# A written-out order searched anew: exponentials over four banks, block 0 normalised by VectorE, 20 leading products

## The chip, the cores and the metric

The kernel runs on one core of a Trainium2 chip. The metric is device time in microseconds of one execution. Every time before the change comes from three timed runs and from one profiled execution of the same program. In the profile PE is TensorE, PEld its weight loads, ACT ScalarE, DVE VectorE, POOL GpSimd and SP SyncE, which issues all the DMAs here.

## The reference

One transformer block on 2048 tokens of width 640, in bfloat16. Attention works in four segments of 512 tokens, with 32 heads of width 20; between the segments runs a compressive memory. Cut to what matters:

```python
h  = x + A(layernorm(x))
h2 = h + silu(layernorm(h) @ w1) @ w2          # w1: 640 x 1728, w2: 1728 x 640

# A: q, k, v = x @ wq, x @ wk, x @ wv, split in heads and in 4 segments of 512
for s in range(4):
    p     = softmax(q_s @ k_s.T / sqrt(20) + causal_mask)
    a_dot = p @ v_s
    a_mem = (phi(q_s) @ M) / (phi(q_s) @ z + 1e-6)   # phi(t) = t + 1 if t > 0 else exp(t)
    o_s   = sigmoid(beta) * a_mem + (1 - sigmoid(beta)) * a_dot
    M += phi(k_s).T @ v_s ;  z += phi(k_s).sum(0)
return concat(o_s) @ wo
```

## The kernel before

Tokens lie in 16 blocks of 128, four to a segment. Every piece of work is a named *task* with the engine instructions that it issues. The function `build` declares all the tasks; then `schedule` walks `ORDER`, a fixed list of 1462 entries, and appends each task to the instruction stream of its engine in the order of the list. Nothing is decided at run time: each engine runs its own stream in order, and a tracker sets the semaphore waits between engines wherever a task reads or overwrites what another one wrote. An entry reads `name/mark:slots`. The slots are the buffers that the task takes, in the order in which it declares them; the mark picks the engine or the form: A ScalarE, D VectorE, G GpSimd, S SyncE, and C the *column form* of a product. Without a mark the task goes to the first engine that it was declared for, which is ScalarE for evictions of PSUM.

A product in the column form (`mms`, line 549) is written as four products of 32 output columns each, side by side in the array; without the mark it is one product of 128 (line 548). The scores (line 946) use row tiles instead: heads are 20 wide, and four heads run in four row strips. The products of probabilities and values (line 994) and of the memory (line 1112) are always in column tiles.

PSUM has eight banks of 512 columns. The names of the tasks, with s the segment, b a block, c a chunk of five:

- `x0`, `x1`, `x2` load blocks 0, 1 and 2 to 3 (line 581); `w_q0` and the like load weights (584). All are in SP's queue, in the order of the list.
- `fill25` is 25 products on zeros that nothing reads (620), `fill5` five more.
- `n1_st`, `n1_rs`, `n1_ap` are the first layer norm of a block: two half-row sums and an aggregation on VectorE (753, 756; block 1's sums are made on ScalarE, 744 to 748), the reciprocal root on GpSimd (763, 765), and the normalising itself, on VectorE (781), for block 0 on ScalarE (777) with a product of mean and root from GpSimd (768) ahead of it. `n1_tp`, `n1_te` transpose blocks 0 to 3 on TensorE and evict them (791, 800); later blocks use a DMA transpose (`n1_tr`, 806).
- `re_q`, `re_k` rearrange the weights of queries and keys (711). `pr{s}{c}{w}` are the projections of queries (w 0) and keys (w 1), `qe` their evictions (876 on ScalarE, 877 on VectorE), `ex`, `pa`, `pb` the function phi (883, 890, 896). `v` and `ve` are the values and their eviction (842 on ScalarE, 843 on VectorE).
- Group g of segment s has the number k = 8s + g, with four heads. `qk{k}a0`, `qk{k}b0`, `qk{k}e0` are *score visits*: the scores of four heads into two pairs of banks. `e{k}a0` and `e{k}a2` are the exponentials of the first and the second pair, 1024 columns each (959), `mk` the causal mask on GpSimd (971), `av` the product with the values, `oe` its eviction (1008 on ScalarE, 1010 on VectorE), `tm`, `td`, `nm`, `ad` the memory part, the transposition, and the normalising (1044 to 1072).
- `kt`, `mz`, `ma`, `mb` update the memory; `vt` gathers the rows of groups 5 to 7.
- `ot`, `wo`, `rs`, `n2_*` are the output projection, the residual and the second layer norm; `h1_{s}_{f}_0.{z}`, `th`, `s` the first layer of the MLP with its activation (1211 on ScalarE, 1217 on VectorE); `h2`, `o`, `out` the second layer, the sum and the store.

The scores and their exponentials as they stand (lines 940 to 962):

```python
sca = [G.alloc("ps", 2) for _ in range(nr // 2)]      # two pairs of banks
...
for q0 in range(r0, r0 + nr, 2):
    scp = sca[(q0 - r0) // 2]
    def e_ex(eng, q0=q0, scp=scp):
        b0 = scp.slot
        T.add(AC, lambda e: e.activation(out=pt[:, pta.slot, q0:q0 + 2, 0:width],
                                         in_=sc3[:, b0:b0 + 2, 0:width], func=ACT.Exp, scale=SCALE), ...)
    G.task(f"e{name}{q0}", {AC: act_c(2 * width)}, e_ex, [(scp, [0])], [(pta, [q0])], ...)
```

## Time and profile before

| | |
|---|---|
| timed runs | 295.88, 297.27, 298.88 us; median 297.27 |
| profiled execution | span 293.9 us from the first to the last instruction; the page gives no time of its own beside the span |
| TensorE busy | 282.0 us, 96% of the span, 4365 products and as many weight loads |
| VectorE, ScalarE, GpSimd busy | 218.6 (74%), 216.5 (74%), 148.1 us (50%) |
| exponentials of the scores | 160, 154.1 us, 1.027 us each |
| granted TensorE clock | full in all 40 slices of the page |
| HBM | read 10.41 MB, written 2.62 MB |

How to read it: "busy" adds up the time in which an engine runs an instruction, over the whole span. A stage in which one engine is full sets its pace by that engine, whatever the mean is; so the stretches of 20 us are read beside the page. A group of instructions shows its line, engine, operation, output and inputs with their shapes, the count, the busy time in all and the mean of one in ns, then the idle time ahead of it and what ended that. "issue" is time in which an engine waited for nothing that the profile shows. Instructions of one engine that follow each other closely overlap a little, so a piece of several is shorter than its count times the mean.

### The profile page before, as it was taken

To read this page: it belongs to the slowest core of one execution; us is meant where nothing else is said; L and a number is where in the kernel's file an instruction comes from. 1 tells how busy PE (TensorE), PEld (TensorE's weight loads), DVE (VectorE), ACT (ScalarE), POOL (GpSimd) and SP (SyncE) were. 2 spreads that over 40 slices of the span, in tenths; PEclk is the share of its full clock that TensorE was granted. 3 is DMA by queue.
4 is the path that set the end of the run, shared out by engine and by line. 5 is a ranking of instruction groups with operands and counts; after the bars stand their busy time and mean duration, and the time that the engine had idled before them with its cause. 6 is when DMAs were issued, how large, how long until landed. Compare 5 with 4: busy or idle time off the path is not lost.

```text
span 293.9 us, 10138 instructions
## 1 busy us (share of the span) xinstructions
PE 282.0 (96%) x4365; PEld 159.8 (54%) x4365; DVE 218.6 (74%) x456; ACT 216.5 (74%) x281; POOL 148.1 (50%) x294
## 2 busy tenths in 40 slices
PE   6899889999999999999999899999999999999996
PEld 5454435445644445566654554656664657754574
DVE  3999888899997678798899835877746776635613
ACT  7699999999999899977789857979979640005400
POOL 6759675686947545746748432348638321300000
PEclk9999999999999999999999999999999999999999
DMA  7947869635464200453543402403320031450003
GB/s 212 342 120 186 113 176 186 167 69 108 87 80 113 73 2 3 53 99 70 91 122 92 93 2 21 81 2 57 73 25 2 2 70 22 91 156 0 3 0 112
DMA packets 48604, 24.83 MB, mean 84 GB/s; under 512 B 38896, under 2 KB 47472, under 8 KB 48560
## 3 DMA queue, kind: packets, MB, share of 16 engines
q1 hardware_dynamic: 48560, 24.19, 38.1%
q8 instruction: 34, 0.56, 0.8%
q14 instruction: 10, 0.08, 0.1%
HBM read 10.41 MB, written 2.62 MB: 44 GB/s over the span
## 4 chain that ended last, share of the span: by engine, by line
PE 83%; DVE 7%; ACT 6%; DMA 1%; issue 1%; POOL 0%; SPq 0%; ACTq 0%; DVEq 0%
PE ps_all L548 49%; PE ps_all L549 20%; PE ps_all L946 8%; ACT PT L959 5%; PE ps_all L994 5%; DMA x_tok<-in_A_x_dram 1%; PE ps_all L1198 1%; DVE xn_rot L781 1%; DVE oTs L1010 1%; DVE phiQ L890 1%; DVE stt L753 1%; PE ps_all L1112 1%; DVE Vx L843 1%; DVE otok L1046 1%; DVE QK L877 0%
## 5 line engine op out<-in xcount | busy, mean ns | idle before, releaser
L959 ACT ACTIVATE PT<-ps_all 128x1024 bf16<-128x1024 f32 x160 | 154.1, 1027 | 16.2 <-PE ps_all L946 15.1
L971 POOL TENSOR_SCALAR_AFFINE_SELECT PT<-PT 128x512 bf16<-128x512 bf16 x128 | 82.8, 651 | 63.9 <-ACT PT L959 60.5
L1211 ACT ACTIVATE th<-ps_all 128x512 f32<-128x512 f32 (+1 forms) x56 | 31.7, 589 | 38.1 <-PE ps_all L548 23.7
L1217 DVE SCALAR_TENSOR_TENSOR sT<-th,ps_all 128x512 bf16<-128x512 f32 (+1 forms) x56 | 36.0, 661 | 17.0 <-ACT th L1211 16.4
L548 PE MATMUL ps_all<-w_sb,sT 128*128 128x320 bf16 x324 | 46.3, 299 | 0.1
L548 PE MATMUL ps_all<-tT,w_sb 128*128 128x512 bf16 x178 | 41.4, 380 | 0.0
L548 PEld LDWEIGHTS ps_all<-w_sb,sT 128*128 128x128 bf16 x324 | 31.0, 98 | 13.2 <-issue 0.6
L753 DVE BATCH_NORM_STATS2 stt<-x_tok 128x6 f32<-128x320 bf16 x62 | 27.1, 478 | 3.8 <-DMA x_tok<-in_A_x_dram 3.6
L1072 POOL TENSOR_TENSOR otok<-on 128x320 bf16<-128x320 bf16 x24 | 19.7, 824 | 17.5 <-DVE on L1064 17.5
L1254 DVE SCALAR_TENSOR_TENSOR x_tok<-ps_all,x_tok 128x640 bf16<-128x640 f32 (+1 forms) x17 | 13.3, 784 | 17.9 <-PE ps_all L548 13.1
L548 PEld LDWEIGHTS ps_all<-tT,w_sb 128*128 128x128 bf16 x178 | 16.5, 98 | 18.7 <-issue 0.6
L877 DVE CAST QK<-ps_all 128x512 bf16<-128x512 f32 x25 | 17.1, 685 | 8.6 <-PE ps_all L548 4.7
L1010 DVE TENSOR_SCALAR oTs<-ps_all,lsc 128x512 bf16<-128x512 f32 x26 | 19.3, 741 | 2.6 <-PE ps_all L994 2.2
L549 PE MATMUL ps_all<-tT,w_sb 128*32 128x512 bf16 x328 | 20.5, 380 | 0.0
L1064 DVE TENSOR_TENSOR on<-ps_all,rd 128x640 bf16<-128x640 f32 x24 | 19.8, 824 | 0.8
L765 POOL TENSOR_TENSOR rst<-rst,eps_c 128x1 f32<-128x1 f32 x32 | 18.3, 573 | 2.5
L549 PE MATMUL ps_all<-w_sb,sT 128*32 128x320 bf16 x496 | 18.8, 300 | 0.0
L781 DVE TENSOR_SCALAR xn_rot<-x_tok,mvt,rst 128x640 bf16<-128x640 bf16 x31 | 16.1, 534 | 3.3 <-POOL rst L765 2.8
L548 PE MATMUL ps_all<-tT,wkr 128*128 128x512 bf16 (+1 forms) x77 | 18.4, 367 | 0.0
L548 PE MATMUL ps_all<-wv_sb,tT 128*128 128x320 bf16 x115 | 18.0, 300 | 0.5 <-ACT PT L959 0.3
L763 POOL TENSOR_TENSOR rst<-mvt,eps_c 128x1 f32<-128x1 f32 x32 | 6.7, 209 | 22.5 <-DVE mvt L756 21.8
L994 PE MATMUL ps_all<-PT,Vx 128*32 128x512 bf16 (+3 forms) x384 | 17.4, 301 | 0.0
(111 smaller groups left out, 403.1 us busy)
## 6 DMA issues: line engine op xcount, KB each, us to landing
out_dram<-x_tok SPq DMA_DIRECT2D x15, 160.0 KB, 1.9
w_sb<-in_B_w_dram SPq DMA_DIRECT2D x5, 432.0 KB, 4.1
x_tok<-in_A_x_dram SPq DMA_DIRECT2D x3, 640.0 KB, 4.4
w_sb<-in_B_w_dram SPq DMA_DIRECT2D x3, 480.0 KB, 4.0
QKV<-QK SPq DMA_DIRECT2D x12, 72.0 KB
wv_sb<-in_A_wv_dram SPq DMA_DIRECT2D x1, 800.0 KB, 8.2
wo_sb<-in_A_wo_dram SPq DMA_DIRECT2D x1, 800.0 KB, 5.3
w_sb<-in_B_w_dram SPq DMA_DIRECT2D x1, 640.0 KB, 6.0
```

The costliest lines, as they stand in the source:

```text
L548: return [lambda e: e.matmul(out, lhsT=lhsT, rhs=rhs, start=start, stop=stop)]
L549: return [lambda e, p=p: e.matmul(out[p:p + 32, :], lhsT=lhsT[:, p:p + 32], rhs=rhs, start=start, stop=stop, tile_position=(0, p)) for p i ...
L753: T.add(DV, lambda e, hh=hh: e.bn_stats(out=stt[:, s, 6 * hh:6 * hh + 6], in_=xb[:, 320 * hh:320 * hh + 320]), reads=R((xa, xsub)), writes ...
L946: fns.append(lambda e, j=j, o=o, r=r, q0=q0, q1=q1, qa=qa, ka=ka: e.matmul(ps_all[:, o:o + q1 - q0], lhsT=ka[32 * r:32 * r + DH, 128 * j:1 ...
L959: T.add(AC, lambda e: e.activation(out=pt[:, pta.slot, q0:q0 + 2, 0:width], in_=sc3[:, b0:b0 + 2, 0:width], func=ACT.Exp, scale=SCALE), re ...
L971: fns.append(lambda e, v=v: e.affine_select(out=v, in_=v, pattern=[[0, 4], [1, 128]], compare_op=ALU.is_ge, fill=0.0, base=0, channel_mult ...
L994: fns.append(lambda e, j=j, r=r, h=h, pa=pa, pt=pt, co=co, q0=q0, ji=ji: e.matmul(bank(po)[32 * r:32 * r + 32, q0:hi], lhsT=vtile(vx)[:, j ...
L1010: f = lambda e: e.tensor_scalar(out=o, in0=i_, scalar1=lsc[:, g:g + 1], scalar2=None, op0=ALU.mult)
L1064: T.add(DV, lambda e: e.tensor_tensor(out=on[:, ona.slot, :, :].rearrange("p b (x e) -> p b x e", e=DH), in0=v[:, :, :, 0:DH], in1=r2.unsq ...
L1072: T.add(PO, lambda e: e.tensor_tensor(out=o_dst, in0=on[:, ona.slot, 0, :].rearrange("p (i x) -> p i x", i=4), in1=on[:, ona.slot, 1, :].r ...
L1211: T.add(AC, lambda e: e.activation(out=th[:, tha.slot, lo:hi], in_=bank(ps)[:, lo:hi], func=ACT.Tanh, scale=0.5), reads=R((ps, [0])), writ ...
L1217: T.add(DV, lambda e: e.scalar_tensor_tensor(out=sT[:, f, lo:hi], in0=th[:, tha.slot, lo:hi], scalar=1.0, in1=bank(ps)[:, lo:hi], op0=ALU. ...
```

## The change

Four edits, none in the arithmetic of the result:

1. `ORDER` is another list of 1448 entries. The tasks are the same.
2. A new mark W. A score visit whose exponential has it runs one activation over its two pairs of banks, 2048 columns, through an address pattern with the distance of the pairs, and the entry of the other half goes. The pairs are taken in the order of their slots, by the scores too. 14 visits have it: e0b0, e7b2, e13a0, e13b2, e14a0, e14b0, e15a0, e16a0, e21a0, e23b0, e24b2, e24e2, e29a2, e29b0.
3. Block 0's normalising has only VectorE's form; ScalarE's, and GpSimd's product for it, are gone.
4. `fill20` stands in the place of `fill25`.

The diff, cut to its core; of the list the start, a part of segment 0, and a part of segment 1:

```diff
 class Graph:  # schedule
-            t.cols = eng == "C"
-            t.eng = {"A": AC, "D": DV, "G": PO, "S": SP, "C": PE}[eng] if eng else list(t.engs)[0]
+            t.cols, t.whole = eng == "C", eng == "W"
+            t.eng = {"A": AC, "D": DV, "G": PO, "S": SP, "C": PE, "W": AC}[eng] if eng else list(t.engs)[0]
             assert t.eng in t.engs and (t.alt or not t.cols)
-            for a in t.allocs:
+            both = [t]
+            if t.whole:
+                m = todo.pop(name[:-1] + ("2" if name[-1] == "0" else "0"))
+                assert not any(self.tasks[p].name in todo for p in m.preds), name
+                both.append(m)
+            for a in [a for q in both for a in q.allocs]:
...
 ORDER = """
-epsc:0 iota halfc zpad warm:0 x0:0 mt2 n1_st0:4 mt3 mt0 mt1 mta1 mtb1 vpad1 x1:1 n1_st1/A:1,2 x2:2,3 w_q0:0 w_q1 w_k0
-vpad0 fill25:0 n1_rs0 n1_ap0/A:1 sel n1_tp0:2 fill5:7 n1_te0/A:1 n1_st2/D:5,3 mta0 n1_rs1 n1_st3:0 n1_rs2 w_k1 w_wv:0
-n1_rs3 re_wk4/G:0 mtb0 mm4 n1_ap1 n1_tp1:0 n1_ap2 n1_tp2:4 n1_ap3:0 n1_tp3:2 re_wq0/D:0 n1_te1/A pr000x.0:6 re_wq0h/D
+zpad:0 warm:0 x2:11,10 halfc iota mt3 epsc mta3 x0:7 n1_st0:6 sel x1:8 n1_st1/A:5,3 n1_rs0 n1_rs1 n1_st2:2,0 n1_rs2
+fill20:1 n1_ap0:1 n1_tp0:3 fill5:7 n1_te0:0 n1_st3:1 n1_rs3 n1_ap1 n1_tp1:6 n1_te1 n1_ap2 n1_tp2:3 n1_te2 w_k0:0
+re_wk0/G:0 w_k1 n1_ap3:1 n1_tp3:0 n1_te3 w_q0 re_wq0:0 pr000x.0/C:5 w_q1 re_wq2/G mt0 mt2 mta0 re_wk3/G re_wq4/G
+re_wq1/A re_wk0h re_wq0h re_wk1 pr001x.0/C:7 pr001x.1/C pr000x.1/C re_wk2 pr001y.0/C:6 pr001y.1/C pr000y.0/C:1
+pr000y.1/C pr011.0/C:2 qe000x:0 qe001x/D qe001y pa001:1 re_wq3 qe000y qk0a0:3,6 pr011.1/C qe011/D:0 ex001:1 beta
+w_wv:0 lsc0 e0a0:4 zf0 zf1 pr010.0/C:0 pr010.1/C qe010/D e0a2 qk0b0:2,4 e0b0/W:0 pr021.0/C:1 pr021.1/C qe021:0
...
+n1_st6:5 ex021:1 ex011:0 vt06:0 kt00:4 vt00 w_w1_4 qk1a0:5,2 e1a0:2 pr041.0:7 pr041.1 qe041/D:0 e1a2 v02.0:4 v02.1
+ve02 qk1b0:1,6 e1b2:5 e1b0 pb011 n1_ap5:3 n1_tr5:1 pa021:0 pb021 n1_ap7:2 mm4 mk0b mk0a mzc4 n1_rs4 n1_ap4:0 vt09
...
+s0_2_0 pa141:2 pb141 qk13a0:0,2 e13a0/W:6 h1_0_4_0.0:5 pr231.0:7 h1_0_4_0.1 th0_4_0:0 s0_4_0 pb140 pr231.1 qe231/D:0
+qk13b0:2,0 e13b2/W:1 h1_0_3_0.0/C:4 h1_0_3_0.1/C th0_3_0:0 mk12a mk12b mk12e av12:5 oe12/D:0 w_w2_1 kt12:1 kt14:3
...
     def layer_norm(tag, b, xa, xsub, dstA, i, prio):
-            if first:
-                T.add(PO, lambda e: e.tensor_scalar(out=nmr[:, s, :], in0=mvt[:, s, 0:1], scalar1=rst[:, s, :], scalar2=-1.0,
-                                                    op0=ALU.mult, op1=ALU.mult),
-                      reads=R((st, ["mv", "r"])), writes=R((st, ["n"])))
...
-            if eng == AC:
-                T.add(AC, lambda e: e.activation(out=xn_rot[:, xn.slot, :], in_=x_tok[:, b % 12, :], func=ACT.Identity,
-                                                 scale=rst[:, s, :], bias=nmr[:, s, :]),
-                      reads=R((xa, xsub), (st, ["r", "n"])), writes=R((xn, [0])))
-                return
...
-        G.task(f"{tag}ap{b}", {DV: 0.46, AC: 0.70} if first else {DV: 0.46}, e_apply,
-               [(xa, xsub), (st, ["mv", "r", "n"] if first else ["mv", "r"])], [(xn, [0])], prio)
+        G.task(f"{tag}ap{b}", {DV: 0.46}, e_apply, [(xa, xsub), (st, ["mv", "r"])], [(xn, [0])], prio)
...
     def scores(name, pool, pt, blocks, pr, width=L, sub=WH):
+                ets = []
+
+                def rank(sca=sca, ets=ets):
+                    if any(t.whole for t in ets):
+                        return sorted(sca, key=lambda a: a.slot)
+                    return sca
...
-                    def e_ex(eng, q0=q0, scp=scp):
+                    def e_ex(eng, q0=q0, scp=scp, rank=rank, ets=ets):
+                        if any(t.whole for t in ets):
+                            a, b = rank()
+                            src = bass.AP(tensor=ps_all, offset=512 * a.slot,
+                                          ap=[[4096, 128], [512 * (b.slot - a.slot), 2], [512, 2], [1, width]])
+                            o = pt[:, pta.slot, 0:4, 0:width].rearrange("p (a b) x -> p a b x", a=2)
+                            T.add(AC, lambda e: e.activation(out=o, in_=src, func=ACT.Exp, scale=SCALE),
+                                  reads=[("ps", z.slot + q) for z in (a, b) for q in range(2)], writes=R((pta, [0, 2])))
+                            return
```

More of the change, by code (lines that the diff above doesn't have):

```diff
@@ L229 @@
     __slots__ = ("name", "engs", "emit", "reads", "writes", "prio", "mode", "allocs", "preds", "npred",
-                 "succ", "ready", "lat", "start", "end", "eng", "idx", "bw", "cols", "alt")
+                 "succ", "ready", "lat", "start", "end", "eng", "idx", "bw", "cols", "alt", "whole")
 class Graph:
@@ L253, in task @@
         t = Task()
-        t.cols, t.alt = False, alt
+        t.cols, t.alt, t.whole = False, alt, False
         t.name, t.emit, t.mode, t.lat, t.bw = name, emit, mode, lat, bw
@@ L318, in schedule @@
             assert not slots, name
-            for a in t.allocs:
-                a.users -= 1
+            for q in both:
+                for a in q.allocs:
+                    a.users -= 1
             order.append(t)
@@ L368 @@
-pr011.0:2 pr011.1 re_wk3/D qe001x/A re_wq4/G qk0a0:0,3 ex001:0 pa001:0 pb001 kt00:2 pr021.0:7 pr021.1 e0a2:4 qe011/D:0
-qe021/D:0 e0a0 pr010.0:6 vpad2 w_w1_0/S pa021:1 n1_st4:3 pr010.1 qe010/D pa011:2 n1_st5:0 ex011:1 pb011 kt01:3
-qk0b0:4,2 w_w1_2/S e0b2:5 e0b0 v00.0/C:0 pr020.0/C:7 pr020.1/C mk0a qe020/A v00.1/C n1_rs5 vt09:0 zf0 vt03 n1_st7:1
-n1_rs7 qk0e0:2,4 v01.0:6 v01.1 e0e2:2 v02.0:4 e0e0 ve01/D:0 zf1 v02.1 n1_ap5:0 n1_tr5:2 ve00/A vt00 qk1a0:6,1 ex021:1
-pr031.0:3 pr031.1 ve02/D n1_st6:7 lsc0 e1a0:1 n1_rs4 n1_ap4:1 e1a2 qe031/D:0 qk1b0:6,4 v03.0:0 lsc1 lsc2 lsc3
@@ new lines @@
+pr101.0/C:4 pr101.1/C e6b0 qk6e0:0,2 e6e2:1 e6e0 mm5 mk5a vpad1 mm7 mm0 mk5b av5:7 mm3 mzc7 mz01:5 n1_tr8 qe101/D mz04
+mz00 mz02 mz03 ma0:0 pr111.0/C:4 qk7a0:5,2 e7a0:3 e7a2 oe5/D:1 pr111.1 qe111/D pr130.0:0 pr130.1 qe130/D:0 qk7b0:4,6
+e7b2/W:0 ex100:1 v13.0/C:1 mk6a mzc0 n1_rs9 n1_ap9:0 mm1 mzc1 mk6e mzc5 mk6b n1_tr11 w_w2_0 w_w1_2 td5/C:3 nm5:3
+w_wo:0 n1_tr9 mk7a v13.1/C ve13/D av6:0 qk8a0:3,5 e8a0:4 e8a2 mk7b oe6/D:0 pa101:1 pr140.0:7 pr140.1 qe140/D:0 av7:4
+oe7/D:1 qk8b0:0,2 e8b0:2 e8b2 mk8b mm6 mb00:0 mk8a td6/C:6 nm6:2 pr131.0/C:7 td7/C:4 nm7:1 qk8e0:5,0 e8e0:6 pr131.1
@@ L509, in build @@
     rst = sb("rst", [128, pools["st"], 1], F32)
-    nmr = sb("nmr", [128, pools["st"], 1], F32)
     eps_c = sb("eps_c", [128, 2], F32)
@@ L733, in layer_norm @@
         xn = G.alloc("xn")
-        first = tag == "n1_" and b < 1
         if tag == "n1_":
```

197 lines of the change are left out of this document (96 added, 101 removed).

## The prediction

> **What bounds the kernel now.** I read the page's engine line first, then the stretches of 20 us. The columns of a stretch are its length, then the busy time of TensorE (PE), its weight loads, VectorE, ScalarE and GpSimd, the granted clock, and the DMA share.
>
> ```profile
> span 293.9 us, 10138 instructions
> PE 282.0 (96%) x4365; PEld 159.8 (54%) x4365; DVE 218.6 (74%) x456; ACT 216.5 (74%) x281; POOL 148.1 (50%) x294
> ...
> 0.00:20.00 20.00, 16.40 (x171) 10.13 (x172) 14.44 (x47) 15.34 (x24) 13.42 (x47) 1.00 0.77 241
> 20.00:40.00 20.00, 17.66 (x258) 8.93 (x256) 17.39 (x40) 19.44 (x25) 15.32 (x34) 1.00 0.69 123
> 40.00:60.00 20.00, 18.98 (x407) 9.16 (x399) 18.12 (x38) 19.33 (x23) 12.90 (x25) 1.00 0.85 188
> 60.00:80.00 20.00, 19.43 (x405) 11.06 (x398) 19.28 (x45) 19.10 (x24) 15.45 (x37) 1.00 0.49 91
> 80.00:100.00 20.00, 19.87 (x383) 9.87 (x385) 16.73 (x33) 18.56 (x25) 12.16 (x21) 1.00 0.50 103
> 100.00:120.00 20.00, 19.84 (x338) 9.40 (x330) 15.41 (x29) 19.25 (x26) 10.98 (x17) 1.00 0.01 3
> ...
> 160.00:180.00 20.00, 18.99 (x285) 10.37 (x278) 13.04 (x28) 14.64 (x21) 7.42 (x14) 1.00 0.23 47
> ...
> 280.00:294.00 14.00, 11.29 (x84) 7.90 (x81) 3.45 (x5) 0.00 (x0) 0.00 (x0) 1.00 0.17 59
> ```
>
> TensorE is busy for 96% of the span. By stretches it lacks 3.6 us of the first twenty, 2.3 of the second, 1.0 of the third, 0.6, 0.1 and 0.2 of the next three, 1.0 at 160 to 180, and 2.7 at the end, where the last output leaves. ScalarE is the engine that is full from 20 to 120 us: 19.4, 19.3, 19.1, 18.6 and 19.3 of 20. So up to some 60 us ScalarE sets the pace and TensorE waits for it; from 60 to 120 us both are full; behind that TensorE alone decides. A new order can win only what TensorE waits, at most 3.4 us between 20 and 60 us and about 2 behind, or less TensorE work.
>
> **TensorE's work.** The chain that ended last shows what a visit costs, and what a change of tiling costs (start, length, then the work).
>
> ```profile
> 42.76 1.19 PE ps_all L549 x20
> ...
> 62.40 1.19 PE ps_all L548 x5
> ...
> 100.17 1.08 PE ps_all L549 x20
> ...
> 104.63 2.27 PE ps_all L549 x40
> ...
> 154.75 2.26 PE ps_all L548 x10
> ```
>
> L548 are full products, L549 the same work in four column tiles (the mark C). Five full products of 512 columns behind other tiling take 1.19 us, ten take 2.26, so 1.07 for five and 0.12 for the change. Twenty column products take 1.19 behind scores and 1.08 behind the value visits, which are column products too; forty take 2.27. Both forms cost the same, and a change of tiling costs 0.11. Counted from the two lists, TensorE runs the same 508 visits beside the filler; 291 instead of 121 of them are in column form, and the changes of tiling fall from 173 to 167: six times 0.11 is 0.7 us less at most. I take 0.6.
>
> [...] The sum keeps equal cost.
>
> **ScalarE's work.** The groups by shape, then one piece of the chain.
>
> ```profile
> L959 ACT ACTIVATE PT<-ps_all 128x1024 bf16<-128x1024 f32 x160 | 154.1, 1027 | 16.2 <-PE ps_all L946 15.1
> ...
> L1211 ACT ACTIVATE th<-ps_all 128x512 f32<-128x512 f32 x52 | 30.3, 604 | 35.6 <-PE ps_all L548 23.7 <-DVE sT L1217 11.4 <-PE ps_all L549 0.4
> ...
> L883 ACT ACTIVATE ex<-QK 128x512 bf16<-128x512 bf16 x25 | 15.5, 630 | 1.2 <-DVE phiQ L896 1.2
> ```
>
> ```profile
> 37.24 3.79 ACT PT L959 x4
> ```
>
> An exponential over 1024 columns takes 1.027 us, one activation over 512 takes 0.604: 0.423 per 512 columns. Four in a row take 3.79, so 0.948 each: 0.08 overlap. Over 2048 columns I estimate 1.027 + 2 x 0.423 = 1.873, and 1.79 in a row, against 1.90 for two: 0.10 less each, 1.4 us for all 14. No row shows four banks in one instruction. At best it saves 0.10; if the address pattern over two pairs cost as much as a start, it saves nothing. I take 0.10. It frees the first pair of banks 0.85 us later; where the lists have such a visit, the next scores on those banks stand behind some 2 us of other products, which cover that. Two of the 14 (e0b0, e7b2) lie before 60 us, where ScalarE decides: 0.2 us. The other twelve lie where TensorE is full; they win between 0 and 1.2, and I take 0.2.
>
> **The start.** The order in time of the first 14 us.
>
> ```profile
> 0.80 1.35 SPq L581 DMA_DIRECT2D x_tok<-in_A_x_dram  x3
> ...
> 1.12 4.32 PE L620 MATMUL ps_all<-zpad 128*128 128x256 bf16 x25 [1.12 <-DVE zpad L599]
> ...
> 3.10 0.89 DVE L753 BATCH_NORM_STATS2 stt<-x_tok 128x6 f32<-128x320 bf16 x2 [2.03 <-DMA x_tok<-in_A_x_dram]
> ...
> 3.59 0.74 ACT L744 ACTIVATE xn_rot<-x_tok 128x640 bf16<-128x640 bf16 x1 [0.23 <-DMA x_tok<-in_A_x_dram]
> ...
> 4.02 0.21 DVE L756 BATCH_NORM_AGGREGATE mvt<-stt 128x2 f32<-128x12 f32 x1
> 4.15 0.17 DVE L642 TENSOR_SCALAR ident<-iot 128x128 bf16<-128x128 int32 x1
> ...
> 5.61 0.92 ACT L777 ACTIVATE xn_rot<-x_tok,nmr,rst 128x640 bf16<-128x640 bf16 x1
> ...
> 5.88 0.88 DVE L753 BATCH_NORM_STATS2 stt<-x_tok 128x6 f32<-128x320 bf16 x2 [1.56 <-DMA x_tok<-in_A_x_dram]
> ...
> 6.58 0.45 PE L791 MATMUL ps_all<-ident,xn_rot 128*128 128x128 bf16 x5 [1.14 <-ACT xn_rot L777]
> ...
> 7.08 0.19 POOL L763 TENSOR_TENSOR rst<-mvt,eps_c 128x1 f32<-128x1 f32 x1 [0.56 <-DVE mvt L756]
> 7.35 0.55 POOL L765 TENSOR_TENSOR rst<-rst,eps_c 128x1 f32<-128x1 f32 x1
> ...
> 9.22 0.45 DVE L781 TENSOR_SCALAR xn_rot<-x_tok,mvt,rst 128x640 bf16<-128x640 bf16 x1 [0.51 <-POOL rst L765]
> ...
> 10.08 0.71 PE L548 MATMUL ps_all<-tT,wqr 128*128 128x256 bf16 x5
> ...
> 13.47 0.39 PE L946 MATMUL ps_all<-w_sb 20*128 20x512 bf16 x4
> ...
> 13.92 1.94 ACT L959 ACTIVATE PT<-ps_all 128x1024 bf16<-128x1024 f32 x2 [0.26 <-PE ps_all L946]
> ```
>
> Now block 0 is in at 3.1 us, block 1 at 3.6, blocks 2 and 3 at 5.9. After the change the double load goes first and block 0 is the third block of four in the same queue: in between 3.6 and 5.9, and I take 4.7; block 1 then ends at 5.9. VectorE's list begins with the sums of block 0 and cannot pass them: 0.89 + 0.21 from 4.7 to 5.8, the identity (0.17) to 6.0, block 2's sums to 7.1. Only then comes the normalising of block 0, now on VectorE (0.45), to 7.5. ScalarE's 0.92 at 5.61 and GpSimd's product ahead of it go. Block 3's sums end at 8.6. Block 1's, on ScalarE, took 3.59 to 5.61 and now run from 5.9 to 7.9; its reciprocal root ends at 8.7, and those of blocks 2 and 3 stand behind it on GpSimd at 0.19 + 0.55 each, to 9.4 and 10.2. So block 3 is normalised at 10.6 instead of 9.67, 0.9 later, and the first projection starts near 11.0 instead of 10.08. The weights aren't late: the key weights take the place of the query weights, and the value weights move behind. The first scores need all four evictions of projection 0; ScalarE has the last transposes and a rearranging (re_wq1, 640 columns, so about the 0.92 of the row at 5.61) ahead of two of them. I walk that to 14.2 for the scores (13.47 now) and 14.7 for the first exponential (13.92): **0.8 us late**. Bounds: 0.3, if block 0 is in at 4.2, and 1.4, if at 5.3.
>
> Then one gap on ScalarE. In the new list the eviction ve02 stands between the second and third exponential of group 1, and its products stand behind the scores qk1a0, pr041 and v02.
>
> ```profile
> 19.34 2.82 PE ps_all L548 x20
> ```
>
> ```profile
> 22.32 0.24 ACT L646 ACTIVATE bsel<-beta_bc 128x32 f32<-128x32 bf16 x1
> ...
> 22.54 3.77 ACT L959 ACTIVATE PT<-ps_all 128x1024 bf16<-128x1024 f32 x4
> ```
>
> Twenty value products take 2.82, so 0.70 a half; five projections 1.08; v02 ends 1.1 + 1.4 = 2.5 us behind qk1a0. ScalarE's two exponentials fill 1.9 (now four run on for 3.77). It idles some 0.6 us, and the two exponentials behind it wait. It can't be below nothing; at most it is 0.9. Up to the ninth group of scores (some 58 us) ScalarE also gets one eviction of 512 columns more (qe021, 0.5) and loses lsc0 (0.2) and one exponential of L883's kind (ex101, 0.5 in a row); with the two joined visits, 0.4 less. So the ninth group is +0.8 + 0.6 - 0.4 = **1.0 us late**. From there TensorE has the same work in both lists, and the delay stays.
>
> The rest I cost at nothing. VectorE and GpSimd swap rearrangings and evictions; VectorE has 17.4 and 18.1 of 20 us between 20 and 60, and its list to that point differs by under 1 us by my count, so if it became the bound it would be late, or early, by as much. SP issues x4, w1_3 and x8 ahead of the first transposed keys, which nothing reads before the memory products behind the sixth group of scores (mz01). Removing five leading products costs TensorE nothing while it waits for block 0; what it costs if that cover is gone is the third rival.
>
> **Instructions.** The column form has four products and four loads where the full form has one.
>
> ```profile
> q8 instruction: 34, 0.56, 0.8%
> ```
>
> ```profile
> 167.53 0.11 PEld L946 LDWEIGHTS ps_all<-QKV 20*128 20x128 bf16 x5 [0.21 <-issue]
> ...
> 168.79 0.10 PEld L946 LDWEIGHTS ps_all<-QKV 20*128 20x128 bf16 x3 [1.15 <-issue]
> ```
>
> The first row is from the page's queues: 34 packets, 0.56 MB, 16 KB each. The program's 4365 products and as many loads come to 8730 instructions; 34 packets are one for each 257. The other two rows are a pause of 0.9 us inside one score visit, with no engine to wait for ("issue", longer than the load's own 0.1): I read it as a late refill. After the change there are 6592 products by my count of the lists, 51 packets, one each 5.5 us instead of 8.3. I take one more pause, 0.9 us; between none and five (4.5).
>
> **Sum.** Start and gap +1.0, tilings -0.6, late joined visits -0.2, refills +0.9, other waits behind 60 us as now: +1.1 us. The profiled execution's span is 293.9, so 295.0 after; the median of the three runs, 297.27, stands 3.3 above the span, and I carry the difference over: 298.4 us.
>
> **Rivals.** (1) **The waits go**: the new list feeds TensorE through its waits. For it: 2.3 and 1.0 us of idle between 20 and 60 us, 1.0 at 160 to 180, and less ScalarE work in that part. Against it: ScalarE is full there, and the late start moves it as a whole. If block 0 is in at 4.2, the gap closes and 3.4 us of waits go: +0.3 - 0.4 - 0.8 - 3.4 = -4.3, 293.0. [...] Five pauses more instead of one: +4.7, 302.0. (3) **The clock falls** between the leading products and the first transposes. The first products ran slower (25 of 256 columns take 4.32 us, 0.17 each; 512 columns take 0.214 later, so 256 take 0.107); the granted clock is 1.00 in every stretch. Twenty end near 4.7, the first transposes come at 7.5: 2.8 us without a product, against 1.1 now. If the clock halves, the projections ahead of the first scores (10.08 to 13.47) take up to 3.4 us longer: +4.5, 301.8. [...] (4) **Joined visits cost as much as two**: +0.4, 298.8, inside the forecast.
>
> [...]
>
> **How the numbers follow.** Forecast 0.57 (with rival 4), waits go 0.16, refills 0.17, clock 0.10. The forecast's own range is 296.0 to 300.5, from its bounds; the whole range reaches to 293.9 and 302.0. One per cent is 3.0 us, about what a measurement can tell from no change: faster is under 294.3, slower over 300.2. Of the forecast 0.03 is over that, so slower is 0.30; of the first rival 0.13 is under it; the rest, 0.57, is within.
>
> **What would show it.** The start: block 0's sums begin at 4.2 to 5.3, first scores near 14.2, first exponential near 14.7. The joined visits: 14 rows of 2048 columns near 1.87 us. ScalarE idles before ve02. TensorE's busy time stays near 282, with 51 instruction packets; pauses marked "issue" inside visits show refills. A clock under full in the first 20 us shows rival 3. I am wrong if TensorE's idle between 20 and 60 us falls under 2 us, or if idle behind 60 us doubles.

## The result, and the profile after

The changed kernel takes 308.11 us in the median (307.73 to 308.59), against 298.07 us (295.88 to 299.03) for the kernel before on the same chip: a ratio of 1.0366, 95% interval 1.0309 to 1.0424. It is 10 to 11 us slower, where I had said 298.4 and no measurable change. The profiled execution spans 306.9 us, 13.0 more than the one before.

From the page of the kernel after: the engine line, the granted clock in 40 slices, and the queue of the instructions.

```profile
span 306.9 us, 14572 instructions
...
PE 285.4 (93%) x6582; PEld 169.4 (55%) x6592; DVE 219.1 (71%) x451; ACT 217.4 (71%) x270; POOL 147.8 (48%) x295
...
PEclk9799986999999999999999999999999999999999
...
q8 instruction: 52, 0.85, 1.2%
```

VectorE, ScalarE and GpSimd are busy within 1 us of before, TensorE for 285.4 us instead of 282.0, with products at half clock among them. What grew most is the time in which TensorE waits, and the clock is no longer full: it is at 7 tenths in the second slice and at 8 and 6 in the sixth and seventh. The stretches of 20 us (length, then the busy time of TensorE, its loads, VectorE, ScalarE and GpSimd, the clock, the DMA share, GB/s):

```profile
0.00:20.00 20.00, 15.48 (x217) 9.50 (x217) 12.35 (x39) 13.67 (x23) 10.62 (x39) 0.91 0.75 245
20.00:40.00 20.00, 17.89 (x267) 9.26 (x264) 18.03 (x44) 18.78 (x24) 14.80 (x34) 1.00 0.54 87
40.00:60.00 20.00, 17.35 (x373) 8.07 (x364) 13.68 (x28) 16.19 (x18) 12.85 (x30) 0.83 0.58 102
60.00:80.00 20.00, 17.18 (x318) 8.93 (x321) 16.32 (x35) 17.34 (x20) 11.76 (x27) 1.00 0.72 152
80.00:100.00 20.00, 17.38 (x415) 10.22 (x405) 17.72 (x36) 17.82 (x25) 13.38 (x27) 1.00 0.59 102
100.00:120.00 20.00, 19.36 (x464) 9.26 (x466) 15.45 (x28) 17.37 (x18) 9.97 (x15) 1.00 0.27 61
```

From 40 to 100 us TensorE lacks 2.7, 2.8 and 2.6 us, where it lacked 1.0, 0.6 and 0.1. ScalarE, full there before, now has 2 to 4 us idle in each. So the two engines no longer hold each other up at full pace: something else ends their waits. The list of what TensorE waited for (us in total, times, longest), six of its rows:

```profile
PE ps_all L786 <- DVE xn_rot L777: 3.3, 3, 1.7
PE ps_all L556 <- issue: 2.1, 3, 1.4
PE ps_all L948 <- DMA QKV<-w_sb: 1.9, 1, 1.9
...
PE ps_all L948 <- DVE Vx L838: 1.1, 1, 1.1
...
PE ps_all L556 <- DMA sT<-otok: 1.0, 1, 1.0
PE ps_all L948 <- issue: 0.7, 2, 0.6
```

and the one row of before that answers to "issue":

```profile
PE ps_all L946 <- issue: 0.9, 1, 0.9
```

Three places carry much of what was lost, and each has its own cause.

**The start.** The order in time of the first 16 us:

```profile
4.34 0.89 DVE L759 BATCH_NORM_STATS2 stt<-x_tok 128x6 f32<-128x320 bf16 x2 [3.27 <-DMA x_tok<-in_A_x_dram]
...
6.97 0.45 PE L786 MATMUL ps_all<-ident,xn_rot 128*128 128x128 bf16 x5 [1.40 <-DVE xn_rot L777]
...
9.67 1.38 PE L786 MATMUL ps_all<-ident,xn_rot 128*128 128x128 bf16 x10 [1.71 <-DVE xn_rot L777]
...
10.78 0.45 DVE L777 TENSOR_SCALAR xn_rot<-x_tok,mvt,rst 128x640 bf16<-128x640 bf16 x1 [0.50 <-POOL rst L771]
...
12.06 0.83 PE L556 MATMUL ps_all<-tT,wqr 128*32 128x256 bf16 x12
...
15.50 0.40 PE L948 MATMUL ps_all<-w_sb 20*128 20x512 bf16 x4
...
15.94 1.02 ACT L969 ACTIVATE PT<-ps_all 128x1024 bf16<-128x1024 f32 x1
```

The first projection starts 2.0 us later than before (10.08), the first exponential too (13.92). Part of it is the clock, which comes next.

**The clock.** The trace tells when the granted clock changes: in the profile after at 9.70, 13.11, 43.83 and 50.66 us, each a whole number of times 3.41 us from the others. Busy time and clock of TensorE (second number, and the clock ahead of the last two) in single periods of 3.41 us between such times:

```profile
6.29:9.70 3.41, 1.03 (x11) 0.72 (x12) 2.04 (x7) 2.35 (x6) 1.44 (x5) 1.00 1.04 365
9.70:13.11 3.41, 3.11 (x38) 2.23 (x41) 2.77 (x10) 2.44 (x5) 3.33 (x11) 0.50 0.78 253
40.42:43.83 3.41, 1.86 (x45) 0.83 (x36) 2.66 (x6) 2.90 (x4) 2.80 (x7) 1.00 0.23 42
43.83:47.24 3.41, 2.49 (x22) 1.06 (x27) 1.44 (x4) 1.94 (x2) 1.56 (x3) 0.50 0.78 184
47.24:50.65 3.41, 3.41 (x31) 0.96 (x31) 2.19 (x6) 2.49 (x3) 2.96 (x9) 0.50 1.12 223
```

A period with TensorE busy for 1.03 of 3.41 us is followed by one at half clock, a period with 1.86 by two. The mean clock of all four timed executions was 0.982 or 0.983, so each had three such periods. In the second case a wait of 1.9 us stands behind it. SyncE's queue and the scores that wait:

```profile
23.91 0.51 SPq L591 DMA_DIRECT2D w_sb<-in_B_w_dram  x1
26.88 1.22 SPq L801 DMA_TRANSPOSE tT<-xn_rot  x1
...
34.30 4.17 SPq L903 DMA_DIRECT2D QKV<-w_sb  x6
38.52 1.20 SPq L801 DMA_TRANSPOSE tT<-xn_rot  x1
39.76 1.36 SPq L903 DMA_DIRECT2D QKV<-w_sb  x2
41.16 2.44 SPq L1111 DMA_TRANSPOSE phiKt<-phiK  x1
...
44.41 0.40 PE L948 MATMUL ps_all<-w_sb 20*128 20x256 bf16 x4 [1.89 <-DMA QKV<-w_sb]
```

Twelve gathers `vt` (L903) must land before `qk4e0` and the groups behind it can run. SyncE issues without a break from 26.88 to 49.3 us, at 0.7 us for a gather and 1.2 for a transpose, and the last gather leaves at 41.1. Ahead of that it stood still from 24.42 to 26.88: its next entry was the transpose of block 5, whose normalising VectorE ends at 26.85 (22.18 before), and only two gathers had left. Before, three had left by 25.6, and the other gathers followed with the last eight in one piece:

```profile
32.51 5.64 SPq L908 DMA_DIRECT2D QKV<-w_sb  x8
```

So the last left at 38.1, and the scores did not wait.

**The pauses.** Three pieces between 67 and 74 us:

```profile
67.78 0.62 PE L556 MATMUL ps_all<-tT,wkr 128*32 128x512 bf16 x8 [1.39 <-issue]
...
69.42 4.70 SPq L1171 DMA_TRANSPOSE sT<-otok  x3
...
73.59 0.59 PE L556 MATMUL ps_all<-wo_sb,sT 128*32 128x320 bf16 x12 [1.04 <-DMA sT<-otok]
```

TensorE stops for 1.39 us inside the projection pr131, with nothing to wait for. A packet of instructions started at 65.50 and took 1.07 us. The transposition td7 behind it comes late, so the DMA transposes (L1171) do, and the output projection waits 1.04 us more.

### The profile page after: what moved, and what is told of

It reads as the page before. It is cut to its first block, busy times and chain, and to the rows that moved or that the text cites. A ratio compares the mean times of both kernels' runs of the same rounds, so it can differ in the third digit from the quotient of the medians.

```text
span 306.9 us, 14572 instructions
## 1 busy us (share of the span) xinstructions
PE 285.4 (93%) x6582; PEld 169.4 (55%) x6592; DVE 219.1 (71%) x451; ACT 217.4 (71%) x270; POOL 147.8 (48%) x295
## 4 chain that ended last, share of the span: by engine, by line
PE 63%; DVE 16%; DMA 9%; ACT 4%; issue 3%; SPq 3%; POOL 1%; ACTq 0%; DVEq 0%
PE ps_all L556 46%; PE ps_all L555 7%; PE ps_all L948 6%; PE ps_all L1004 3%; DMA x_tok<-in_A_x_dram 3%; DVE stt L759 3%; DVE xn_rot L777 3%; ACT PT L969 2%; SPq L903 2%; DMA tT<-otok 1%; DMA sT<-otok 1%; DMA phiKt<-phiK 1%; DMA QKV<-w_sb 1%; DVE sT L1227 1%; DVE x_tok L1186 1%
## 5 line engine op out<-in xcount | busy, mean ns | idle before, releaser
L969 ACT ACTIVATE PT<-ps_all 128x1024 bf16<-128x1024 f32 x132 | 127.7, 1026 | 21.2 <-PE ps_all L948 20.6
L556 PE MATMUL ps_all<-w_sb,sT 128*32 128x320 bf16 x1536 | 55.7, 299 | 0.0
L556 PE MATMUL ps_all<-tT,w_sb 128*32 128x512 bf16 x860 | 51.9, 379 | 0.7 <-issue 0.7
L556 PEld LDWEIGHTS ps_all<-w_sb,sT 128*32 128x32 bf16 x1536 | 41.6, 97 | 11.3 <-issue 1.6
L556 PEld LDWEIGHTS ps_all<-tT,w_sb 128*32 128x32 bf16 x860 | 22.3, 97 | 18.8 <-issue 2.4
L965 ACT ACTIVATE PT<-ps_all 128x2048 bf16<-128x2048 f32 x14 | 26.3, 1878 | 2.6 <-PE ps_all L948 2.5
L556 PE MATMUL ps_all<-wv_sb,tT 128*32 128x320 bf16 x480 | 18.7, 300 | 0.0
L556 PE MATMUL ps_all<-wo_sb,tT 128*32 128x320 bf16 x480 | 18.1, 299 | 0.7 <-DMA tT<-otok 0.7
L556 PE MATMUL ps_all<-tT,wqr 128*32 128x512 bf16 (+1 forms) x276 | 18.1, 388 | 0.1
L556 PE MATMUL ps_all<-tT,wkr 128*32 128x512 bf16 (+1 forms) x264 | 16.6, 368 | 1.4 <-issue 1.4
```

Of the source, the lines that this page charges most:

```text
L556: return [lambda e, p=p: e.matmul(out[p:p + 32, :], lhsT=lhsT[:, p:p + 32], rhs=rhs, start=start, stop=stop, tile_position=(0, p)) for p i ...
L965: T.add(AC, lambda e: e.activation(out=o, in_=src, func=ACT.Exp, scale=SCALE), reads=[("ps", z.slot + q) for z in (a, b) for q in range(2) ...
```

## The experiments

Every ratio below is to the kernel before on the same chip, with its 95% interval; the changed kernel stands at 1.0366. In the diffs only entries of `ORDER` change, and "..." stands for entries left as they are.

### First: the queue, the clock and the start

Theory 1 was the late gathers and the clock they cost; theory 2 that ScalarE sets the pace anyway. **a_queue** moves entries of SyncE only:

```diff
-vt06:0 kt00:4 vt00 w_w1_4 ... n1_tr5:1 ... vt09 kt02:3 n1_tr4 vt03 n1_tr7 ... vt02 n1_tr6 vt010 vt07 qk4e0:2,0
+vt06:0 kt00:4 vt00 vt09 vt03 ... n1_tr5:1 ... kt02:3 n1_tr4 n1_tr7 ... vt02 vt010 vt07 n1_tr6 w_w1_4 qk4e0:2,0
```

> The changed kernel with only SyncE's queue of the first segment reordered: the gathers vt09 and vt03 go ahead of the transpose n1_tr5, and the transpose n1_tr6 and the weight load w_w1_4 behind the last gather vt07. Theory 1 (the last gathers stand too late in that queue, TensorE waits for them ahead of the scores qk4e0, and this idle time drops its clock for two periods): the wait of 1.97 us at 44.4 us goes, the half clock from 43.8 to 50.7 us goes with it (some 2.8 us), 4 to 5 us less, about 303.5 us. Theory 2 (ScalarE sets the pace up to there and the wait only shows its delay): under 1 us less, 307 to 308. If the wait goes and the clock falls all the same: about 306.

Measured: 305.86 us (304.43 to 306.65), 1.0288 (1.0225 to 1.035). The last gathers and the scores:

```profile
36.65 2.04 SPq L902 DMA_DIRECT2D QKV<-w_sb  x3
...
42.48 0.29 PE L947 MATMUL ps_all<-w_sb 20*128 20x256 bf16 x4
```

The last gather leaves at 38.7 and the scores have no wait. Two of the gathers now run where the queue had stood still. That is 2.3 us less, half of what theory 1 gave, and what the third branch gave (about 306): the wait of 1.9 went, but the four executions still had mean clocks from 1.00 down to 0.983, and pauses of 0.2 and 0.6 us stand inside visits at 53 and 63 us. A difference of two ratios is less certain than either: the 2.3 us are known to 2.5 us either way, so they are not clear of nothing.

**b_filler** leaves the queue and fills the wait:

```diff
-vt07 qk4e0:2,0
+vt07 fill18:2 qk4e0:2,0
```

> The changed kernel with 18 products of zeros (256 columns each, some 1.9 us at full clock) put on TensorE ahead of the scores qk4e0, where it waits 1.97 us; the queue order is as it was. Theory 1 with the clock as a cost of its own: the wait stays, the half clock from 43.8 to 50.7 us goes, 2.5 to 3 us less, about 305.3. Rival (the half clock costs nothing, since the other engines are behind anyway): 308, as the changed kernel.

Measured: 306.70 us (304.94 to 308.06), 1.0317 (1.0232 to 1.0402). In its profile the clock stays full from 15.9 us on, with the gathers as late as in the changed kernel (at the start two periods are at half clock here, where the changed kernel had one). The mean clocks of the four executions, 0.988 to 0.994, leave one or two periods at half clock instead of three. So with the wait filled the clock is 1.00 from 43.5 to 50.3 us, where the changed kernel had 0.50 from 43.83 on. The gain, 1.5 us, is smaller than its interval.

**c_start** lengthens the leading products:

```diff
-fill20:1 n1_ap0:1 n1_tp0:3 fill5:7
+fill30:1 n1_ap0:1 n1_tp0:3 fill16:7
```

> The changed kernel with 30 leading products instead of 20 and 16 instead of 5 between the first transposes, so that TensorE is busy from 1 to 9 us. If the first fall of the clock (half from 9.7 to 13.1 us) comes from the idle time behind the 20 products: the clock stays full, the first scores start near 14.8 instead of 15.50 and 0.7 us is won at the start; carried to the end 307.4, swallowed by the later wait for the gathers 308. If the fall doesn't depend on it: the half clock stays and the time is 308 or a little over.

Measured: 305.29 us (304.66 to 307.03), 1.0283 (1.0219 to 1.0347). TensorE's first two periods at full clock:

```profile
5.18:8.59 3.41, 3.19 (x32) 2.66 (x31) 2.73 (x10) 2.60 (x6) 1.81 (x6) 1.00 1.01 315
8.59:12.00 3.41, 2.70 (x59) 2.02 (x60) 2.69 (x10) 2.41 (x5) 2.86 (x9) 1.00 1.04 339
```

The first fall is gone, and 2.5 us with it, more than I gave it, though known to 2.6 us either way only. In this profile the second fall is there, one period long, behind the same wait.

**i_queue_start** has both edits.

> Both edits, the reordered queue and the longer leading products. If the two causes are separate and the delay is carried to the end: their sum, some 5 us less, about 302.7, with the clock full throughout. If one swallows the other: as the better of the two alone.

Measured: 305.17 us (303.12 to 307.41), 1.0272 (1.019 to 1.0353), 2.8 us less (known to 3.0 either way), not 5. The clock is full throughout in the profile, and the wait at `qk4e0` is gone. So theory 1 is right on the wait and the clock, but queue, start and clock together are about a quarter of the loss here. The profile still has pauses: TensorE stopped inside visits at 51, 54, 63 and 107 us, for 0.3 to 1.5 us each.

### Second: one part of the change at a time

**d_two_exp** takes the joined visits apart (`e0b0/W:0` becomes `e0b0:0 e0b2`, and so for all 14).

> The changed kernel with its 14 joined visits taken apart again, two exponentials of 1024 columns each, in the same places. By rows of 1.878 us for the joined one and 1.03 each (0.95 in a row) for the two: nothing to 1.4 us more, 308 to 309.5. A rival that the joined instruction holds its four banks too long and costs time: under 307.

Measured: 306.61 us (305.68 to 307.55), 1.0339 (1.0295 to 1.0383): 0.8 us less, inside the interval.

**e_full_rows** drops every mark C (`pr000x.0/C:5` becomes `pr000x.0:5`).

> The changed kernel with every column-tiled visit turned back into full products: the same order, 2947 products instead of 6592. If instruction refills cost the changed kernel much (52 packets of instructions): half as many packets, the pause of 1.4 us at 66 us gone, 1.5 to 4 us less, 304 to 306.5. If column form and full form cost the same and only the changes of tiling count: the count of changes decides, 0.1 us each, and the time goes up by some us, since the value visits then stand between full products.

Measured: 303.88 us (302.63 to 304.26), 1.0239 (1.0196 to 1.0282): 3.8 us less, the most of any single edit so far, although every value visit now stands between full products and pays two changes of tiling (0.11 us each by the rows of before). The page has 23 packets of instructions, and the pause at 66 us is gone.

**h_dve_norm** is the list of before with block 0 on VectorE (`n1_ap0/A:1` becomes `n1_ap0:1`).

> The list of before, but block 0 normalised by VectorE instead of ScalarE: that part of the change alone. VectorE has 0.45 us more between the sums of blocks, ScalarE 0.92 less. My step: costs nothing, 298 within 0.5. Rival (VectorE's list sets the start): 0.4 to 0.5 us more.

Measured: 296.90 us (295.57 to 298.65), 0.9994 (0.996 to 1.0028). That part of the change costs nothing, to within 1 us.

**g_joined_before** joins 39 visits in that list (`e0b2:5 e0b0` becomes `e0b2/W:5`).

> The list of before with block 0 on VectorE, and 39 visits joined, all those whose two exponentials follow each other and whose four banks lie side by side. At 0.10 us saved for each where ScalarE sets the pace (20 to 60 us, some 8 visits) and where both engines are full (60 to 120 us): 0.8 to 2 us less than the same list without the joining, 296 to 297.3. Rival (the banks come free later and TensorE waits for them): 1 to 3 us more, 299 to 301.

Measured: 309.37 us (308.93 to 311.84), 1.0449 (1.0394 to 1.0504): 12 to 14 us more than h_dve_norm (by the medians and by the ratios), far beyond the rival's 3. ScalarE's exponentials and the scores around 43 us in this kernel:

```profile
43.37 1.88 ACT L961 ACTIVATE PT<-ps_all 128x2048 bf16<-128x2048 f32 x1
45.31 0.39 PE L944 MATMUL ps_all<-QKV 20*128 20x512 bf16 x4 [0.42 <-ACT PT L961]
45.76 1.02 ACT L965 ACTIVATE PT<-ps_all 128x1024 bf16<-128x1024 f32 x1 [0.50 <-PE ps_all L944]
```

and in h_dve_norm:

```profile
40.37 6.61 ACT L966 ACTIVATE PT<-ps_all 128x1024 bf16<-128x1024 f32 x7
...
43.68 0.40 PE L945 MATMUL ps_all<-QKV 20*128 20x512 bf16 x4
```

With separate exponentials TensorE fills the first two banks again while ScalarE reads the next two, and seven exponentials run on without a gap. A joined one holds all four banks to its end, 1.88 us; the next scores wait 0.42 us for it, then ScalarE waits 0.50 us for them. In the list of waits of g_joined_before, TensorE waits 12.0 us for joined exponentials (L961); this is the longest row:

```profile
PE ps_all L944 <- ACT PT L961: 7.3, 12, 1.2
```

In h_dve_norm the rows of waits for exponentials add up to 2.0 us.

### Third: fewer instructions

**j_thin** keeps the changed order, but gives the column form only to those visits where it saves a change of tiling; chosen by counting the changes over the whole stream.

```diff
-pr000x.0/C:5 ... pr001x.0/C:7 pr001x.1/C pr000x.1/C ... h1_3_2_0.0/C:7 ... h2_15_0/C:2
+pr000x.0:5 ... pr001x.0:7 pr001x.1 pr000x.1 ... h1_3_2_0.0:7 ... h2_15_0:2
```

> The changed kernel with the same order, but the column form only where it saves a change of tiling: 127 visits in column form instead of 291, 163 changes of tiling instead of 167, 4483 products instead of 6592. Theory 3 (TensorE's own instruction refills cost the changed kernel several pauses, not the one that I took): some 35 packets of instructions instead of 52, the pause of 1.4 us near 66 us gone, and with it the late transposes behind; 3 to 6 us less than the changed kernel, 302 to 305, and less than the all-full version, which pays for more changes of tiling. Rival (the pauses hide beside other waits, and the queue of SyncE alone is the cause): under 1.5 us less, 306.5 to 308.

Measured: 306.06 us (302.69 to 306.52), 1.0243 (1.0196 to 1.0291). By the ratio 3.7 us less; by the median only 2, for the profiled execution at 302.69 was the fastest of six and the others lie from 305.2 up. So by the ratio it lies in theory 3's range of 3 to 6 us less, by the median between the two branches. It has 35 packets, but still two long pauses, of 1.6 and 1.4 us.

**k_all** puts four edits together (thinned columns, queue, joined visits taken apart, `fill26` and `fill12`).

> The changed kernel with four edits: few column-tiled visits as above, the reordered queue, the 14 joined visits taken apart, and 26 leading products with 12 between the first transposes. If the causes are separate: what remains is the late start of about 1 us and the waits of the list from 60 to 140 us, some 3 to 4 us more than before, 299.5 to 302. If one cause lies behind all of them: no less than the best single one, 303 to 305.

Measured: 300.14 us (298.70 to 301.37), 1.0076 (1.0044 to 1.0109): 8.6 us of the 10.9 are back (known to 2.0 either way), more than any edit alone gave. All ten executions had a mean clock of 0.999 or more.

**l_before_thin** thins the columns in the list of before (with block 0 on VectorE), and **m_before_start** also lengthens its second filler:

```diff
-fill25:0 n1_rs0 n1_ap0/A:1 sel n1_tp0:2 fill5:7
+fill25:0 n1_rs0 n1_ap0:1 sel n1_tp0:2 fill12:7
```

> The list of before with block 0 on VectorE and the column form only where it saves a change of tiling: 82 visits instead of 121, 164 changes instead of 173, 3900 products instead of 4365. At 0.11 us a change 1.0 us less, and some four packets of instructions fewer with perhaps one pause: 295 to 296.5. If fewer instructions are worth as much as theory 3 gives for the changed kernel (0.15 us a packet): 295.5. If neither shows: 297.

> The same as the list of before with few column-tiled visits, and 12 instead of 5 products of zeros between the first two transposes, so that TensorE doesn't idle from 7 to 9 us. If the clock falls there in some executions and costs 1 to 2 us when it does: a narrower spread and 0.5 to 1 us less than without the products, 294.5 to 296. If the fall doesn't depend on them: the same.

Measured: 297.67 us (295.86 to 299.99), 0.9995 (0.9959 to 1.0031), and 296.83 us (295.85 to 298.56), 0.9966 (0.9931 to 1.0). Neither is shown to beat the kernel before; the second is the best version here, at most 0.7% ahead. Nine changes of tiling fewer should have given 1.0 us; in the profile of l_before_thin one pause of 1.5 us stands in a visit (at 50 us) where before had none, and eight of its twelve executions had a mean clock of 0.994, against four of twelve with the longer filler, which may be chance.

### Fourth: what stays of the combined kernel

**n1_joined_back** joins the 14 visits again, **n2_columns_back** gives all 291 visits the column form again.

> The combined kernel (few column-tiled visits, reordered queue, longer filler) with its 14 joined visits left joined. If joining costs by itself (four banks held for 1.88 us, where the first two came free after 1.03): 0.3 us for each of 14, 3 to 5 us more than the combined kernel, 303.5 to 305. If it costs nothing, as my step had it: 299.5 to 300.5.

> The combined kernel with all 291 visits in column form again, joined visits taken apart. If refills carry the difference between the changed kernel and its thinned form: 3 to 5 us more than the combined kernel, 303 to 305. If queue, filler and joining carried it: under 1 us more, 300 to 301.

Measured: 300.42 us (298.30 to 302.42), 1.0118 (1.0084 to 1.0153), and 304.06 us (302.67 to 307.18), 1.0219 (1.017 to 1.0267). So where the list was made for it the joining costs about 1.2 us, not clear of nothing (known to 1.4 either way), and the columns cost 4.2 us (known to 1.7). The waits of TensorE named "issue" in the combined kernel:

```profile
PE ps_all L552 <- issue: 0.8, 2, 0.5
```

and with all columns back, with the longest pause, which the trace puts down to ScalarE for its end:

```profile
PE ps_all L555 <- issue: 2.1, 5, 0.6
...
PE ps_all L554 <- issue: 1.1, 7, 0.2
...
PE ps_all L947 <- issue: 0.6, 1, 0.6
```

```profile
57.00 0.10 PEld L554 LDWEIGHTS ps_all<-tT,wkr 128*128 128x128 bf16 x1 [1.48 <-issue]
57.22 0.38 PE L554 MATMUL ps_all<-tT,wkr 128*128 128x512 bf16 x1 [1.71 <-ACT PT L968]
```

Its load itself waited 1.48 us for nothing and went on 2.9 us after a packet of instructions had started at 54.12. Without the row of waits of 0.2 us at most, which I take for places where the record of a product is missing (the profile has 6595 products to 6605 loads), that is 4.4 us of pauses (2.1, 0.6 and 1.7) against 0.8, 3.6 more. The times differ by 4.2; but the two profiled executions, the slowest of their kernels (307.18 and 301.37 us), differ by 5.8 us, of which TensorE's idle time makes 5.2. So the pauses carry most of it, not all.

**n3_x0_first** puts the loads in the order of before (`x0 x1 x2` instead of `x2 x0 x1`); **n4_ve23** moves the eviction ve23 to ScalarE (`ve23/D` becomes `ve23/A`).

> The combined kernel with the loads in the order of before, blocks 0 and 1 first and then the double load of 2 and 3. If the order of the loads is what makes the start late: the first transposes 0.5 to 1.2 us earlier and as much less at the end, 299 to 299.6. If GpSimd's and VectorE's chain of statistics sets it: the same, 300.

> The combined kernel with the eviction ve23 on ScalarE instead of VectorE. TensorE waits 1.24 us for it ahead of the scores qk12a0. If VectorE's backlog from 70 to 87 us is a cost of its own: 0.8 to 1.2 us less, 299 to 299.4. If ScalarE or the next wait takes its place: the same, 300.

Measured: 299.35 us (298.50 to 300.73), 1.0071 (1.0045 to 1.0096), and 301.29 us (299.79 to 301.87), 1.0123 (1.0082 to 1.0164). Against the combined kernel the first is the same within 1.2 us, though its first scores start at 13.57 us instead of 14.63: a microsecond won at the start isn't seen at the end, so the order of the loads isn't what is left. Nor is it VectorE's backlog: in n4_ve23 the scores wait as long as in the combined kernel (1.18 us there), now for ScalarE.

```profile
84.52 0.40 PE L944 MATMUL ps_all<-QK 20*128 20x512 bf16 x4 [1.17 <-ACT Vx L833]
```

The list gives these scores the bank that the value product has just filled, so whichever engine evicts it, the scores wait. The last 2.3 us between the combined kernel and before (0.0044 to 0.0109 of the time) I did not take apart further; waits of this kind, written into the list from 80 to 140 us, are my reading of its profile, not shown by a run.

Three of these runs take the edits off one after another. By the ratios the thinned columns give 3.7 us (j_thin), then the queue with the longer filler 3.7 (n1_joined_back against j_thin, known to 1.8, so clear of nothing), then the joined visits 1.2 (the combined kernel), and 2.3 are left, of 10.9. By the medians the first two are 1.5 and 5.1, since j_thin's ratio leans on its one execution at 302.69. The sizes also depend on the order: in the changed list with all its columns, queue and filler gave 2.8 (i_queue_start), and the columns gave 4.2 when they went last.

## Why the prediction was wrong, point by point

**TensorE's work: the price right, the gain not shown.** The column form costs the same in the visit: in the profile after, 42 full products of 512 columns on one weight matrix take 10.4 us and 860 column products 51.9, so 1.24 us for five full ones and 1.21 for twenty columns. Where the stream is dense, from 240 to 300 us, where nearly all products are columns, TensorE's idle time is under 0.5 us in each 20 us. That six changes of tiling fewer gave 0.6 us no run shows; in l_before_thin nine fewer gave nothing measurable.

**ScalarE's work: the price right, the gain not.** From the groups of instructions: 1.878 us for 2048 columns, where I had 1.873.

```profile
L965 ACT ACTIVATE PT<-ps_all 128x2048 bf16<-128x2048 f32 x14 | 26.3, 1878 | 2.6 <-PE ps_all L948 2.5
```

But there is no gain of 0.10 us a visit to be seen: by d_two_exp and n1_joined_back joining costs 0.8 and 1.2 us in all, neither clear of nothing. That the first banks come free 0.85 us later was covered, or nearly, in the 14 places of the new list; in 39 visits of the list of before (eight of the same visits among them) it wasn't, and cost some 13 us.

**The start: right in kind, 0.8 us against 2.0.** Block 0 was in at 4.34 (4.7 taken). Two things made it later. GpSimd's reciprocal roots take 0.8 to 0.9 us each, not the 0.74 of the two rows added up, and block 1's starts at 8.20, so block 3 is normalised at 11.23, not 10.6. And the clock: transposes and first projections between 9.70 and 13.11 ran at half speed. Where a longer filler kept it full, the first scores started at 13.88 (c_start), 14.11 (i_queue_start) and 14.63 (the combined kernel), around the 14.2 of the forecast, instead of 15.50; so most of what the start was late beyond the forecast goes with the clock. The third rival had named just this fall, with a chance of 0.10, my own estimate, on a gap of 2.8 us without a product. There was no such gap: TensorE waited 1.40 us ahead of the first transposes and 1.71 ahead of the next. What went ahead of the fall is a period of 3.41 us with 1.03 us of work.

**The gap ahead of ve02: right.** ScalarE waits 0.59 us, where I had 0.6.

```profile
26.19 0.71 ACT L837 ACTIVATE sT<-ps_all 128x640 bf16<-128x640 f32 x1 [0.59 <-PE ps_all L555]
```

**"The rest I cost at nothing": the step that failed first.** I looked at what SyncE issues ahead of the transposed keys and at who reads these, and not at the gathers behind them in the same queue, which the last scores of the fifth group read. The queue stands still for 2.5 us at a transpose whose block VectorE normalises 4.7 us later than before, and is then full for 22 us, so each entry ahead of a gather makes it later by its own issue, 0.7 to 1.2 us. Undone, the wait goes, and in the profile of a_queue its half clock; with the start that is 2.8 us in the changed list and 3.7 in the thinned one, where I had 0 for the queue and 0.8 for the start.

**Refills: right that they grow, mis-sized.** 52 packets came, 51 were counted. I took one more pause of 0.9 us from one pause in 34 packets. The pauses ("issue", the two rows quoted) grew from 0.9 to 2.8 us in the profile after and to 4.4 in n2_columns_back, and one of them set off a further wait of 1.04 us. With and without the columns, the time differs by 3.7 to 4.2 us by the ratios (j_thin, e_full_rows, n2_columns_back), where the sum had 0.9; that is close to the 4.5 that I had as an upper bound and left to the rival. The five pauses behind that bound and behind the 302.0 were an estimate of mine that no run shows; what the runs show is the 2.8 and 4.4 us. That these pauses are refills was a reading of one row then. The traces bear it out for the long ones: they stand at fixed places of the instruction stream, about one packet apart (the last section). No run changes the number of instructions alone, so that the column form costs only by its refills is argued. Most packets come without such a pause: one of over 0.8 us to 52 packets in the profile after. The eleven pauses of 0.8 us or more in the traces (the last section) all stand in column products, scores or value products; the one at 57.00 us in n2_columns_back, whose end the trace puts down to ScalarE, stands in a full one.

**"From there TensorE has the same work, and the delay stays": failed.** TensorE's idle time from 60 to 120 us went from 0.9 to 6.1 us; that it might double was the sign I had named for being wrong. Behind 20 us both lists have the same work, but the order of before leaves TensorE hardly a wait there, and the new one leaves many. Nor does a delay at the start simply stay: n3_x0_first starts its scores a microsecond earlier and ends no earlier. Of the 2.3 us left in the combined kernel the cause stays open.

**The rivals.** I priced the refills and the clock each alone, at 302.0 and 301.8, with the forecast's other terms kept. Both came together, and with the queue they nearly add up: taken off one after another, 3.7 us for the columns, 3.7 for queue, start and clock, 1.2 for the joining, 2.3 left open, of 10.9 us.

## What to carry to other kernels

Ask of every queue that an edit touches what the *last* entry is, who reads it and how much slack it has; SyncE's issued without a break for 22 us here, and each entry ahead of a gather made it later by 0.7 to 1.2 us. Where a form of instruction costs the same time in more instructions, give it only to the places that it pays for: here four times the products took the same time in a visit (1.21 us against 1.24) and cost some 4 us over the stream. And rivals that don't exclude each other are to be added up before the range is drawn.

## What the hardware showed that I had not expected

**Ahead of each fall stood a period with little work, not one long gap.** Over the profiles of this case the clock was halved nine times after it had been full (a fall within the last microsecond of a span, as at 306.66 us in the profile after, isn't counted), each time after a period of 3.41 us in which TensorE was busy for 29 to 55% of the time (30 and 55% in the profile after). Of the over 1200 full periods that a full one followed, the emptiest had 43, 48, 48, 51 and 54%; between 43 and 55% both are seen, so this share alone doesn't decide it. The longest single wait in the nine periods was 1.2 to 2.3 us, and one of 1.9 us stands in a period that no fall followed. The periods aren't tied to the start of the kernel: one starts at 6.29 us in the profile after and at 5.18 in c_start. Nor does the same kernel fall in every execution: of 65 timed executions of the kernel before that lie within 1.5% of the fastest, 50 had a mean clock of 0.999 or more and took 296.9 us in the mean, 15 had one period at half clock (0.993 or 0.994) and took 299.1. One such period goes with 2.2 us here, and with more than half of what these times scatter by.

**The long pauses stood at fixed counts of instructions; their length varied.** Counted in weight loads of TensorE and the semaphore instructions among them, a pause stands behind 1006 or 1007 in the changed kernel (979 loads and 27 others, at 67.78 us) and in a_queue, b_filler, c_start, d_two_exp, i_queue_start and n2_columns_back, though its length is 0.5 to 1.7 us for the load; others stand behind 747 or 748 and behind 876 or 877 in several of these. That is 129 or 130 apart, with as many products about the 257 instructions of one packet. The products of zeros count too: with 21 more of them at the start of c_start the work behind is shifted by 21 against these places, so its pauses fall in other visits, at 55 and 64 us instead of 66, one of 1.82 us:

```profile
57.13 0.40 PE L555 MATMUL ps_all<-tT,wkr 128*32 128x512 bf16 x3 [1.82 <-issue]
```

In all eleven pauses of 0.8 us or more (waits of a product marked "issue", over all profiles of this case), TensorE went on 2.3 to 2.9 us after a packet of instructions had started, while packets start some 6 us apart (52 in the 306.9 us of the profile after). Shorter ones, like the 0.6 us at 98.3 us in the profile after, 4.0 us behind their packet, needn't be refills. So 21 products more at the start went with later pauses in other visits, one of them of 1.82 us.
